# Decode with cached attention: nine VectorE instructions a head in place of fifteen

## The chip, the core and the metric

The kernel runs on one core of a Trainium2 chip. Its time is the device time of one execution, in microseconds (us). The runs of the kernel before took 715.30, 715.63 and 715.83 us: the median is 715.63 us. Lower is better.

In the text, PE is the matrix engine (TensorE), DVE is VectorE, ACT is ScalarE, POOL is GpSimd and SP is SyncE, which issues the loads here. A load is a DMA; 16 DMA engines carry it.

## The reference

One token for each of four sequences (B = 4) goes through two blocks, twice with the same weights: attention on a cache, then a dense MLP with ReLU. All is float32. Cut to what matters:

```python
def _A_ref(x, k_cache, v_cache, wq, wo):          # 32 heads of 128, window W = 1024
    q = (x @ wq).reshape(B, 1, 32, 128).transpose(0, 2, 1, 3)
    k = k_cache[:, :, Sk - W:, :]; v = v_cache[:, :, Sk - W:, :]
    p = softmax(einsum("bhqd,bhkd->bhqk", q, k) * 128 ** -0.5)
    o = einsum("bhqk,bhkd->bhqd", p, v)
    return o.transpose(0, 2, 1, 3).reshape(B, 1, 32 * 128) @ wo

def _B_ref(x, w1, w2):                            # 640 -> 1728 -> 640
    return einsum("bsf,fd->bsd", maximum(einsum("bsd,df->bsf", x, w1), 0), w2)

x = x + _A_ref(layernorm(x), ...);  x = x + _B_ref(layernorm(x), w1, w2)
x = x + _A_ref(layernorm(x), ...);  x = x + _B_ref(layernorm(x), w1, w2)
```

Each head of each pass needs its own part of `wq`, keys, values and its part of `wo`, 4.85 MB, and each is used for one token a sequence only. 302.7 MB are read from HBM in all.

## The kernel before, in words

**Records and slots.** The host packs what a head needs into one record of 9472 floats on each of 128 partitions: query weights (WQ, 640 columns), keys (K, 4096), values (V, 4096), output weights (WO, 640). On the chip five slots (`slot`) hold one record each; a buffer `ring` of 6912 columns holds MLP weights and some pieces of records between the two passes; `kept` holds a last part of one record. The small tiles (`qT`, `of_batch`, `of_block`, `pick`, `mrt`, `small`) are allocated ahead of the slots. Every tile starts at a multiple of 32 bytes in its partition; in the built program slot 0 starts at byte 3072, and the slots, the ring and `kept` at multiples of 256.

**Loads.** All weights are loaded by the SP queue, in one order that `items` holds, written out by hand (`piece`, `ending`, `IN_RING`, `places`). `pump` issues the next load as soon as the place that it overwrites has been marked as read by `done`; since the queue is in order, a load that must wait holds back those behind it. What frees a slot is the head's last use of it, `project`.

**The order of the work.** Every engine's instructions run in the order in which the code states them (`InOrder`). A pass `r` goes over 32 heads. `center` and `query` start it. Then, for each head `n`: `scores` of the next head (8 matrix products over 512 columns, on PE), its `softmax`, `values` of this head (8 products), `picks`, `query` of the head after next, `output_T`, `project` into the accumulator `acc`, and `weights` of the next head. The last heads of a pass stand outside the loop and work by halves. `busy` issues matrix products whose result is not used. Then `center` and `mlp`. In pass 0 the MLP's weights come through the ring: the fifth piece of `w1` overwrites the first, and the pieces of `w2` follow. In pass 1 they lie in two slots.

**VectorE's part of one head (15 instructions).** Four sequences stand on partitions 0, 32, 64 and 96. `softmax`: the row maximum over 1024 scores, its product with `rstd` (1/std of the layernorm); ScalarE then takes the exponential in place with `rstd` as scale, and the sum `tot`. `weights`: the sum is transposed, inverted and spread over the four columns of `mrt` (3 instructions); then, for each half of 512 columns, a transpose by blocks of 32 from `sc_ps` into `t_ps`, and a product that picks one column in each block, times `mrt`, into `wT` (4 instructions). `picks`: the values' product is a [128, 512] tile of which each row needs one of four blocks of 128; `of_block` holds a one in that block's column, and four instructions add the four blocks times their columns. Then the copies of the query (`qT`) and of the transposed output (`oTs`).

**1/std.** `deviation` sums the squares on PE, picks each row's value, sums and takes the root on ScalarE; in a pass it is issued behind the first half of the first head's scores, and in the MLP behind the first piece of `w1`.

In the profile every instruction but a few has line L89 (L86 for an engine's first): it is the line of the helper `InOrder` that calls the engine. So rows are told apart by their tiles.

Of the kernel before, what the change touches and what calls it, by code (L numbers as in the profile page):

```python
# [32 lines left out]
F32 = mybir.dt.float32  # L33
AF = mybir.ActivationFunctionType
OP = mybir.AluOpType
AX = mybir.AxisListType
PSUM = bass.MemoryType.PSUM

P = 128
B, D, H, DH, W, FF = 4, 640, 32, 128, 1024, 1728  # L40
# [56 lines left out]
def decode_kernel(ctx: ExitStack, tc: tile.TileContext, xf, rec, w1, w2, out):  # L97
    nc = tc.nc
    pe, dve, act, pool, sp = (InOrder(tc, e) for e in (nc.tensor, nc.vector, nc.scalar, nc.gpsimd, nc.sync))
    sb = ctx.enter_context(tc.tile_pool(name="sb", bufs=1))  # L100
# [4 lines left out]
    wT = scratch[:, :128].rearrange("p (i c j) -> p i c j", i=2, c=16)  # L105
    on = [scratch[:, 128:256], scratch[:, 288:416]]
# [5 lines left out]
    oTs = sb.tile([P, LATE, B], F32, name="oTs")  # L112
    qT = sb.tile([P, B], F32, name="qT")
    of_batch = sb.tile([P, B], F32, name="of_batch")
    of_block = sb.tile([P, 4], F32, name="of_block")
    pick = sb.tile([P, B], F32, name="pick")
    mrt = sb.tile([P, B], F32, name="mrt")
    small = sb.tile([P, 14], F32, name="small")
    nmax, rtot, rstd, eps, eps_dh, ones, unused, sums, tot0, tot1 = (small[:, i:i + 1] for i in range(10))
    squares = small[:, 10:]  # L120
    tot = [tot0, tot1]
# [4 lines left out]
    sc_ps = [ps.tile([P, W], F32, name=f"sc_ps{i}") for i in range(2)]  # L126
    t_ps = ps.tile([P, 512], F32, name="t_ps")
    o_ps = ps.tile([P, 512], F32, name="o_ps")
    acc = ps.tile([P, 512], F32, name="acc")
    misc = ps.tile([P, 512], F32, name="misc")  # L130
    outs = [o_ps, sc_ps[0][:, 512:]]
# [56 lines left out]
    hs = order[0]  # L188
# [13 lines left out]
    hs = order[1]  # L202
# [10 lines left out]
    for buf, lo, hi in places:  # L213
        while stream:
            h, c, end = stream[0]
# [11 lines left out]
    n = 0  # L227
# [18 lines left out]
    def cols(key, lo, n):  # L246

        for x, y, buf, col in pieces(key):
            if x <= lo and lo + n <= y:
                return buffers[buf][:, col + lo - x:col + lo - x + n]  # L250
        raise KeyError((key, lo, n))
# [39 lines left out]
        dve.tensor_tensor(spread[:, :KB * B].rearrange("p (k b) -> p k b", b=B), blocks, blocks, op=OP.mult)  # L291
        dve.tensor_reduce(squares, spread[:, :KB * B].rearrange("p (k b) -> p b k", b=B), op=OP.add, axis=AX.X)

    def deviation(rows, bias, scale):

        pe.matmul(o_ps[:, 8:8 + B], ones.to_broadcast([P, P]), squares, start=True, stop=True)
        dve.tensor_tensor(mrt, o_ps[:, 8:8 + B], rows, op=OP.mult)
        dve.tensor_reduce(sums, mrt, op=OP.add, axis=AX.X)
        act.activation(rstd, sums, AF.Sqrt, bias=bias, scale=scale / D)

    def xblock(k):
        return xT[:, 32 * k:32 * k + B]

    def query(r, h):
        key = ("rec", r, h)
        for k in range(KB):
            pe.matmul(misc[:, 8:8 + B], cols(key, WQ + k * DH, DH), xblock(k), start=(k == 0), stop=(k == KB - 1))
        done(key, WQ, K)
        dve.tensor_copy(qT, misc[:, 8:8 + B])

    def scores(r, h, s, first=False):
        key = ("rec", r, h)
        for i in range(2):
            for b in range(B):
                pe.matmul(sc_ps[s][32 * b:32 * b + 4, 512 * i:512 * i + 512], qT[:, b:b + 1].to_broadcast([P, 4]),
                          cols(key, K + 512 * (B * i + b), 512), start=True, stop=True)
            done(key, K + VH * i, K + VH * i + VH)
            if first and i == 0:
                deviation(of_batch, eps_dh, float(DH))
                act.activation(unused, eps, AF.Exp)  # L320

    def softmax(s, first=False):

        dve.tensor_reduce(nmax, sc_ps[s], op=OP.max, axis=AX.X, negate=True)
        if first:
            dve.reciprocal(rstd, rstd)
        dve.tensor_tensor(nmax, nmax, rstd, op=OP.mult)
        act.activation(sc_ps[s], sc_ps[s], AF.Exp, bias=nmax, scale=rstd, accum_out=tot[s])

    def weights(s, parts=(0, 1)):  # L330
        if 0 in parts:

            dve.transpose(spread, tot[s].to_broadcast([P, 32]))
            dve.reciprocal(rtot, spread[:, 0:1])
            dve.tensor_scalar(mrt, of_batch, rtot, None, op0=OP.mult)
        for i in parts:
            dve.transpose(t_ps, sc_ps[s][:, 512 * i:512 * i + 512])
            dve.tensor_tensor(wT[:, i], t_ps.rearrange("p (c j) -> p c j", j=32)[:, :, :B],
                              mrt.unsqueeze(1).to_broadcast([P, 16, B]), op=OP.mult)

    def values(r, h, last=False, fill=(0, 0)):
        key = ("rec", r, h)
# [6 lines left out]
                busy(512, misc)  # L349

    def picks(last):
        o, on_ = outs[last], on[last]
        dve.tensor_scalar(on_, o[:, :DH], of_block[:, 0:1], None, op0=OP.mult)
        for c in range(1, 4):
            dve.scalar_tensor_tensor(on_, o[:, DH * c:DH * c + DH], of_block[:, c:c + 1], on_, op0=OP.mult, op1=OP.add)

    def output_T(i, last=False, by_act=False):
        pe.matmul(outs[last][:, :B], on[last], pick, start=True, stop=True)
        if by_act:
            act.copy(oTs[:, i], outs[last][:, :B])  # L360
        else:
            dve.tensor_copy(oTs[:, i], outs[last][:, :B])

    def project(r, h, i, end):
        key = ("rec", r, h)
# [5 lines left out]
    def mlp(r):  # L371


        h_ps, front = sc_ps[0][:, :512], t_ps[:, :224]
        for k in range(KB):
            for j in range(NB):
                pe.matmul(h_ps[32 * j:32 * j + B, :FQ], xblock(k), cols(("w1", r), k * FF + FQ * j, FQ),
                          start=(k == 0), stop=(k == KB - 1))
            done(("w1", r), k * FF, k * FF + FF)
            if k == 0:  # L380
                deviation(pick, eps, 1.0)
                dve.reciprocal(rstd, rstd)
            elif k < KB - 1:
                busy(512)
        act.activation(front, h_ps[:, :224], AF.Relu, scale=rstd)
        act.activation(back[:, :208], h_ps[:, 224:FQ], AF.Relu, scale=rstd)
        act.activation(back[:, 240:], h_ps[:, 416:FQ], AF.Relu, scale=rstd)
        busy(512)
        busy(256)
        dve.transpose(scratch[:, :224], front)  # L390
        dve.transpose(scratch[:, 224:], back)
        key = ("w2", r)
        sizes = W2_SLOT if r else [size for name, size, _ in MLP_RING if name == "w2"]
        first = 0
        for i, size in enumerate(sizes):
            for s in range(first, first + size):
                m, n = TILES[s]
                w = cols(key, s * FD, FD)
                for part, q in ((m, n),) if m < 13 else ((13, n), (14, n + 2)):
                    pe.matmul(acc[32 * q:32 * q + B, :FD], hT[:, part, :B], w,  # L400
                              start=False, stop=(s >= len(TILES) - NB), skip_group_check=True)
            if r == 0 and i < len(sizes) - 2:
                busy(512)
            done(key, first * FD, (first + size) * FD)
            first += size
# [4 lines left out]
    for r in range(2):  # L410
        hs = order[r]
        late = LATE if r == 0 else 2
        center(2 * r)
        query(r, hs[0])
        if r:
            busy(256, groups=2)
        scores(r, hs[0], 0, True)
        softmax(0, True)
        query(r, hs[1])
        weights(0)  # L420
        for n, h in enumerate(hs[:-2]):
            i = n - (H - late)
            s = (n + 1) % 2
            scores(r, hs[n + 1], s)
            softmax(s)
            values(r, h)
            picks(0)
            query(r, hs[n + 2])
            if r and n < NS - 2:
                busy(256, sc_ps[n % 2], 2, H - 1)  # L430
            output_T(max(i, 0))
            if i < 0:
                project(r, h, 0, False)
            weights(s, (0, 1) if n < H - 3 else (0,))
        scores(r, hs[-1], 1)
        softmax(1)
        weights(0, (1,))
        values(r, hs[-2], 0, (0, 1))
        weights(1)
        picks(0)  # L440
        values(r, hs[-1], 1, (1, 0))
        output_T(late - 2, by_act=True)
        picks(1)
        for i in range(late - 3) if late > 2 else (0,):
            project(r, hs[H - late + i], i, False)
        if late == 2:
            busy(512, misc)
        output_T(late - 1, True)
        dve.memset(pad, 0.0)
        for i in (late - 3, late - 1, late - 2) if late > 2 else (1,):  # L450
            project(r, hs[H - late + i], i, i == late - 2 or late == 2)
        center(1)
        mlp(r)
# [40 lines left out]
```

## Time and profile before

| | before |
|---|---|
| runs, us | 715.30, 715.63, 715.83 |
| span of the profiled execution, us (its time around the span is not listed) | 713.9 |
| PE busy | 518.8 us (73%) |
| VectorE busy, instructions | 357.4 us (50%), 1007 |
| ScalarE busy, instructions | 93.3 us (13%), 147 |
| DMA | 303.38 MB, mean 425 GB/s over the span |
| mean granted clock of PE | 0.790 of full speed |

How to read it: the span runs from the first to the last instruction. A group's row has line, engine, operation, what it writes and reads, the shapes, and the count; then its busy time in us and the mean of one in ns; then the idle time of the engine just ahead of it and what ended that. A row of the timeline begins with its start and its length in us. A window's row has, for each engine, busy us and instructions, then PE's granted clock, the busy share of the 16 DMA engines, and GB/s. A row of waits has the total us, the number of waits and the longest. A row of the chain has a start, a length, and the work that the end of the program was waiting for at that time.

### The profile page before, as it was taken

The page shows a single profiled execution, that of the slowest core. Times are in us where ns is not written, and L with a number is a line of the kernel's source. Part 1 is how long each engine was busy: PE and PEld are TensorE (multiplying, and loading weights), DVE is VectorE, ACT ScalarE, POOL GpSimd, SP SyncE. Part 2 cuts the span into 40 slices and gives each one's busy share as a digit, 9 for nine tenths or more (in the row PEclk, how much of TensorE's full clock was granted, in tenths as well). Part 3 has the DMA queues.
Part 4 walks back from the last instruction along what each step waited for, and adds up shares of the span by engine and source line. Part 5 has one row for each costly group of instructions (what it writes and reads, how often), then busy time and mean ns, then how long its engine had stood idle before and what let it go on. Part 6 is the DMA issues. An engine that isn't in the chain of part 4 may idle for free.

```text
span 713.9 us, 8959 instructions
## 1 busy us (share of the span) xinstructions
PE 518.8 (73%) x3716; PEld 210.9 (30%) x3716; DVE 357.4 (50%) x1007; ACT 93.3 (13%) x147; POOL 1.1 (0%) x9
## 2 busy tenths in 40 slices
PE   4466858666785766868889998477767767686868
PEld 2131323223232231323224343132222313232323
DVE  3335445544454545446642887535444454445752
ACT  1201010110110101011111222101010110101111
POOL 0000000000000000000000000000000000000000
PEclk9768686877678677577899999857886687668989
DMA  9999999999999999999999999999999999999996
GB/s 374 442 437 430 425 436 440 429 419 442 438 432 423 434 438 437 417 442 422 424 406 408 428 429 429 442 438 423 430 439 436 427 430 434 437 430 423 429 424 274
DMA packets 16633, 303.38 MB, mean 425 GB/s; under 512 B 1856, under 2 KB 2384, under 8 KB 6736
## 3 DMA queue, kind: packets, MB, share of 16 engines
q1 hardware_dynamic: 16560, 302.80, 99.0%
q8 instruction: 29, 0.48, 0.2%
q14 instruction: 12, 0.10, 0.0%
q10 hardware_dynamic: 32, 0.01, 0.0%
HBM read 302.72 MB, written 0.08 MB: 424 GB/s over the span
## 4 chain that ended last, share of the span: by engine, by line
DMA 79%; PE 17%; DVE 2%; issue 1%; SPq 0%; ACT 0%
DMA slot<-rec 76%; PE sc_ps L89 6%; PE misc L89 5%; PE o_ps L89 4%; DMA ring<-w 3%; PE acc L89 3%; DVE scratch L89 1%; DVE oTs L89 1%; DVE small L89 0%; SPq L89 0%; DVE t_ps L89 0%; SPq L86 0%; DVE xT L89 0%; ACT oTs L89 0%; DVE qT L89 0%
## 5 line engine op out<-in xcount | busy, mean ns | idle before, releaser
L89 PE MATMUL misc<-xT,slot 128*128 128x4 f32 x630 | 103.2, 291 | 154.5 <-DMA slot<-rec 154.3
L89 PE MATMUL sc_ps<-slot,qT 128*4 128x512 f32 x1008 | 196.7, 920 | 1.0 <-DVE qT L89 1.0
L89 PEld LDWEIGHTS misc<-xT,slot 128*128 128x128 f32 x630 | 97.7, 240 | 210.8 <-DMA slot<-rec 199.1
L89 ACT ACTIVATE sc_ps<-sc_ps,small 128x1024 f32<-128x1024 f32 (+1 forms) x68 | 76.6, 1127 | 555.3 <-DVE small L89 554.8
L89 PE MATMUL o_ps<-slot,scratch 128*16 128x512 f32 x964 | 135.1, 672 | 3.0 <-DVE scratch L89 3.0
L89 DVE TENSOR_REDUCE small<-sc_ps 128x1 f32<-128x1024 f32 x64 | 78.3, 1223 | 73.9 <-PE sc_ps L89 73.9
L89 DVE STREAM_TRANSPOSE t_ps<-sc_ps 128x512 f32<-128x512 f32 x128 | 93.2, 728 | 2.1
L89 DVE COPY qT<-misc 128x4 f32<-128x4 f32 x64 | 10.2, 160 | 166.1 <-PE misc L89 166.1
L89 PEld LDWEIGHTS o_ps<-slot,scratch 128*16 128x16 f32 x964 | 32.7, 117 | 128.4 <-issue 79.0
L89 DVE SCALAR_TENSOR_TENSOR scratch<-o_ps,of_block,scratch 128x128 f32<-128x128 f32 x186 | 65.2, 351 | 6.6
L89 PEld LDWEIGHTS sc_ps<-slot,qT 128*4 128x4 f32 x1008 | 33.5, 115 | 84.1 <-issue 73.1
L89 PE MATMUL acc<-slot,oTs 128*4 128x160 f32 x488 | 36.5, 387 | 14.3 <-DVE oTs L89 14.0
L89 DVE TENSOR_SCALAR scratch<-o_ps,of_block 128x128 f32<-128x128 f32 x62 | 21.7, 351 | 34.1 <-PE o_ps L89 34.1
L89 PE MATMUL o_ps<-pick,scratch 128*128 128x4 f32 x124 | 29.1, 305 | 4.8 <-DVE scratch L89 4.8
L89 DVE TENSOR_TENSOR scratch<-t_ps,mrt 128x64 f32<-128x64 f32 x128 | 28.8, 225 | 4.7
L89 PEld LDWEIGHTS o_ps<-pick,scratch 128*128 128x128 f32 x124 | 26.1, 260 | 8.8 <-DVE scratch L89 7.5
L89 PE MATMUL sc_ps<-slot,small 128*1 128x256 f32 (+2 forms) x56 | 17.7, 462 | 0.0
L89 DVE COPY oTs<-o_ps 128x4 f32<-128x4 f32 x60 | 9.7, 162 | 14.8 <-PE o_ps L89 13.9
L89 DVE TENSOR_SCALAR mrt<-of_batch,small 128x4 f32<-128x4 f32 x64 | 14.7, 230 | 2.2
L89 DVE STREAM_TRANSPOSE scratch<-small 128x32 f32<-128x32 f32 x64 | 12.9, 201 | 2.4 <-ACT sc_ps L89 2.4
L89 PEld LDWEIGHTS acc<-slot,oTs 128*4 128x4 f32 x488 | 6.9, 84 | 19.5 <-DVE oTs L89 19.1
L89 ACT ACTIVATION_READ_ACCUMULATOR sc_ps<-sc_ps,small 128x1 f32 x64 | 12.2, 191 | 0.0
(71 smaller groups left out, 113.6 us busy)
## 6 DMA issues: line engine op xcount, KB each, us to landing
slot<-rec SPq DMA_DIRECT2D x43, 4736.0 KB, 30.7
slot<-rec SPq DMA_DIRECT2D x12, 2368.0 KB, 29.6
slot<-rec SPq DMA_DIRECT2D x2, 4416.0 KB
slot<-rec SPq DMA_DIRECT2D x2, 2304.0 KB, 18.4
ring<-w SPq DMA_DIRECT2D x5, 864.0 KB, 10.7
slot<-rec SPq DMA_DIRECT2D x2, 2112.0 KB, 19.0
slot<-rec SPq DMA_DIRECT2D x2, 2048.0 KB, 41.4
slot<-rec SPq DMA_DIRECT2D x4, 1024.0 KB, 20.3
```

The costliest lines, as they stand in the source:

```text
L89: r = build(*args, **kwargs)
```

## The change

Per head, VectorE gets 9 instructions where it had 15:

- `weights` transposes the whole row of 1024 in place in `sc_ps` and makes one product of all 32 blocks. The last two heads of a pass still go by halves, in place as well. `t_ps` is no longer used here.
- `picks` makes one product of the [128, 4, 128] view with `of_block`, in place in PSUM, and one sum over the four blocks.
- 1/std is multiplied into the query (`rrow`, one value a sequence, the same on all partitions) when it is copied to `qT`, for all heads of a pass but the first, whose query is copied ahead of the root. So the product on the row maximum falls away for them, and the exponential's scale is 1. `deviations` replaces `deviation` in attention: the root on four columns, its reciprocal, and the pick of each row's value for the first head.
- All copies to `oTs` are ScalarE's (before: two of them).

The new tile `rrow` has 16 bytes a partition and stands ahead of `small` and the slots. In the built program VectorE has 316 instructions fewer, its waits included, and ScalarE 60 more; PE's matrix products, their order, and the SP queue's loads are the same ones in the same order. The slots, the ring and `kept` start 32 bytes further.

```diff
+    rrow = sb.tile([P, B], F32, name="rrow")
     small = sb.tile([P, 14], F32, name="small")
...
+    def deviations():
+        pe.matmul(o_ps[:, 8:8 + B], ones.to_broadcast([P, P]), squares, start=True, stop=True)
+        act.activation(rrow, o_ps[:, 8:8 + B], AF.Sqrt, bias=eps_dh, scale=float(DH) / D)
+        dve.reciprocal(rrow, rrow)
+        dve.tensor_tensor(mrt, rrow, of_batch, op=OP.mult)
+        dve.tensor_reduce(rstd, mrt, op=OP.add, axis=AX.X)
...
-    def query(r, h):
+    def query(r, h, first=False):
...
-        dve.tensor_copy(qT, misc[:, 8:8 + B])
+        if first:
+            dve.tensor_copy(qT, misc[:, 8:8 + B])
+        else:
+            dve.tensor_tensor(qT, misc[:, 8:8 + B], rrow, op=OP.mult)
...
         dve.tensor_reduce(nmax, sc_ps[s], op=OP.max, axis=AX.X, negate=True)
         if first:
-            dve.reciprocal(rstd, rstd)
-        dve.tensor_tensor(nmax, nmax, rstd, op=OP.mult)
-        act.activation(sc_ps[s], sc_ps[s], AF.Exp, bias=nmax, scale=rstd, accum_out=tot[s])
+            dve.tensor_tensor(nmax, nmax, rstd, op=OP.mult)
+        act.activation(sc_ps[s], sc_ps[s], AF.Exp, bias=nmax, scale=rstd if first else 1.0, accum_out=tot[s])
...
-        for i in parts:
-            dve.transpose(t_ps, sc_ps[s][:, 512 * i:512 * i + 512])
-            dve.tensor_tensor(wT[:, i], t_ps.rearrange("p (c j) -> p c j", j=32)[:, :, :B],
-                              mrt.unsqueeze(1).to_broadcast([P, 16, B]), op=OP.mult)
+        for i, j in parts:
+            half = sc_ps[s][:, 512 * i:512 * j]
+            dve.transpose(half, half)
+            dve.tensor_tensor(wT[:, i:j].rearrange("p i c j -> p (i c) j"),
+                              half.rearrange("p (c j) -> p c j", j=32)[:, :, :B],
+                              mrt.unsqueeze(1).to_broadcast([P, 16 * (j - i), B]), op=OP.mult)
...
     def picks(last):
-        o, on_ = outs[last], on[last]
-        dve.tensor_scalar(on_, o[:, :DH], of_block[:, 0:1], None, op0=OP.mult)
-        for c in range(1, 4):
-            dve.scalar_tensor_tensor(on_, o[:, DH * c:DH * c + DH], of_block[:, c:c + 1], on_, op0=OP.mult, op1=OP.add)
+        o = outs[last].rearrange("p (c d) -> p c d", c=4)
+        dve.tensor_tensor(o, o, of_block.unsqueeze(2).to_broadcast([P, 4, DH]), op=OP.mult)
+        dve.tensor_reduce(on[last], o.rearrange("p c d -> p d c"), op=OP.add, axis=AX.X)
...
-        if by_act:
-            act.copy(oTs[:, i], outs[last][:, :B])
-        else:
-            dve.tensor_copy(oTs[:, i], outs[last][:, :B])
+        act.copy(oTs[:, i], outs[last][:, :B])
...
-            weights(s, (0, 1) if n < H - 3 else (0,))
+            weights(s, ((0, 2),) if n < H - 3 else ((0, 1),))
```

More of the change, by code (lines that the diff above doesn't have):

```diff
@@ L292, in center, with deviation @@
         dve.tensor_reduce(squares, spread[:, :KB * B].rearrange("p (k b) -> p b k", b=B), op=OP.add, axis=AX.X)
-    def deviation(rows, bias, scale):
+    def deviation():
         pe.matmul(o_ps[:, 8:8 + B], ones.to_broadcast([P, P]), squares, start=True, stop=True)
-        dve.tensor_tensor(mrt, o_ps[:, 8:8 + B], rows, op=OP.mult)
+        dve.tensor_tensor(mrt, o_ps[:, 8:8 + B], pick, op=OP.mult)
         dve.tensor_reduce(sums, mrt, op=OP.add, axis=AX.X)
-        act.activation(rstd, sums, AF.Sqrt, bias=bias, scale=scale / D)
+        act.activation(rstd, sums, AF.Sqrt, bias=eps, scale=1.0 / D)
+        dve.reciprocal(rstd, rstd)
+    def deviations():
[4 more added lines that the diff above has]
+        dve.tensor_reduce(rstd, mrt, op=OP.add, axis=AX.X)
     def xblock(k):
         return xT[:, 32 * k:32 * k + B]
-    def query(r, h):
+    def query(r, h, first=False):
         key = ("rec", r, h)
@@ L318, in scores @@
             if first and i == 0:
-                deviation(of_batch, eps_dh, float(DH))
+                deviations()
                 act.activation(unused, eps, AF.Exp)
@@ L325, in softmax, with weights @@
         if first:
-            dve.reciprocal(rstd, rstd)
-        dve.tensor_tensor(nmax, nmax, rstd, op=OP.mult)
-        act.activation(sc_ps[s], sc_ps[s], AF.Exp, bias=nmax, scale=rstd, accum_out=tot[s])
-    def weights(s, parts=(0, 1)):
-        if 0 in parts:
+            dve.tensor_tensor(nmax, nmax, rstd, op=OP.mult)
+        act.activation(sc_ps[s], sc_ps[s], AF.Exp, bias=nmax, scale=rstd if first else 1.0, accum_out=tot[s])
+    def weights(s, parts=((0, 2),)):
+        if parts[0][0] == 0:
             dve.transpose(spread, tot[s].to_broadcast([P, 32]))
@@ L351, in picks, with output_T @@
     def picks(last):
-        o, on_ = outs[last], on[last]
-        dve.tensor_scalar(on_, o[:, :DH], of_block[:, 0:1], None, op0=OP.mult)
-        for c in range(1, 4):
-            dve.scalar_tensor_tensor(on_, o[:, DH * c:DH * c + DH], of_block[:, c:c + 1], on_, op0=OP.mult, op1=OP.add)
-    def output_T(i, last=False, by_act=False):
+        o = outs[last].rearrange("p (c d) -> p c d", c=4)
+        dve.tensor_tensor(o, o, of_block.unsqueeze(2).to_broadcast([P, 4, DH]), op=OP.mult)
+        dve.tensor_reduce(on[last], o.rearrange("p c d -> p d c"), op=OP.add, axis=AX.X)
+    def output_T(i, last=False):
         pe.matmul(outs[last][:, :B], on[last], pick, start=True, stop=True)
-        if by_act:
-            act.copy(oTs[:, i], outs[last][:, :B])
-        else:
-            dve.tensor_copy(oTs[:, i], outs[last][:, :B])
+        act.copy(oTs[:, i], outs[last][:, :B])
     def project(r, h, i, end):
@@ L380, in mlp @@
             if k == 0:
-                deviation(pick, eps, 1.0)
-                dve.reciprocal(rstd, rstd)
+                deviation()
             elif k < KB - 1:
@@ L413, in decode_kernel @@
         center(2 * r)
-        query(r, hs[0])
+        query(r, hs[0], True)
         if r:
@@ L433, in decode_kernel @@
                 project(r, h, 0, False)
-            weights(s, (0, 1) if n < H - 3 else (0,))
+            weights(s, ((0, 2),) if n < H - 3 else ((0, 1),))
         scores(r, hs[-1], 1)
         softmax(1)
-        weights(0, (1,))
+        weights(0, ((1, 2),))
         values(r, hs[-2], 0, (0, 1))
-        weights(1)
+        weights(1, ((0, 1), (1, 2)))
         picks(0)
         values(r, hs[-1], 1, (1, 0))
-        output_T(late - 2, by_act=True)
+        output_T(late - 2)
         picks(1)
```

## The prediction

> **What bounds the kernel now.** I read the page first (the slices, the DMA queues), then the SP queue's waits and the chain that ended last, then windows and the timeline of the two places where that chain leaves the DMA.
>
> ```profile
> span 713.9 us, 8959 instructions
> DMA  9999999999999999999999999999999999999996
> DMA packets 16633, 303.38 MB, mean 425 GB/s; under 512 B 1856, under 2 KB 2384, under 8 KB 6736
> q1 hardware_dynamic: 16560, 302.80, 99.0%
> q8 instruction: 29, 0.48, 0.2%
> q14 instruction: 12, 0.10, 0.0%
> ...
> slot<-rec SPq DMA_DIRECT2D x43, 4736.0 KB, 30.7
> ```
>
> The 16 DMA engines are busy in every slice but the last, and the loads of q1 take 99.0% of their time. A whole record (4736 KB, 4.85 MB) needs 11.4 us at 425 GB/s but lands 30.7 us after its issue: some 19 us of other loads stand in front of it. So the order to load may come many microseconds later or earlier in the body without the DMA engines noticing.
>
> ```profile
> SPq L89 <- PE acc L89: 465.9, 51, 25.2
> ...
> 74.71 31.02 DMA slot<-rec
> ...
> 371.33 0.95 PE sc_ps L89 x8
> 372.30 7.20 DMA ring<-w
> ...
> 707.14 3.87 PE acc L89 x112
> 711.04 0.33 DVE scratch L89
> ```
>
> The first row (the SP queue's waits) says what issues loads: SP waits 465.9 us for a head's last projection, which frees its slot. The others are the chain: 31 us pieces of DMA through both passes of attention, a stretch between the two passes where the ring is fed by loads that land after only 7 us, and from 707 us on PE, DVE, the end. These two stretches are the places where VectorE could matter:
>
> ```profile
> core 0: us, PE busy (x) PEld busy (x) DVE busy (x) ACT busy (x) POOL busy (x), PEclk, DMA share, GB/s
> 369.00:372.00 3.00, 2.54 (x20) 0.51 (x20) 0.48 (x3) 1.58 (x2) 0.00 (x0) 1.00 0.93 364
> 372.00:375.00 3.00, 2.69 (x16) 0.36 (x11) 0.00 (x0) 0.00 (x0) 0.00 (x0) 1.00 0.99 402
> ...
> 706.00:708.00 2.00, 2.00 (x39) 1.24 (x41) 0.87 (x2) 1.02 (x3) 0.00 (x0) 1.00 0.53 220
> 708.00:710.00 2.00, 2.00 (x67) 1.90 (x61) 0.00 (x0) 0.00 (x0) 0.00 (x0) 1.00 0.28 108
> ```
>
> ```profile
> 667.83 1.90 PE L89 MATMUL sc_ps<-slot,qT 128*4 128x512 f32 x16
> ...
> 681.16 9.03 SPq L89 DMA_DIRECT2D slot<-w  x4
> ...
> 710.51 0.11 PEld L89 LDWEIGHTS acc<-slot,scratch 128*4 128x4 f32 x8 [0.18 <-DMA slot<-w]
> ```
>
> In 369 to 372 the DMA share falls to 0.93: the first MLP's fifth piece of w1 overwrites the first, so its load waits until PE has used that, and the queue runs nearly dry. At 7% of 3 us plus 1% of the next 3 this costs 0.24 us. At the end (the second and third row of the timeline) the last four loads are issued by 690.2, long before they are moved; their last piece reaches PE at 710.5, and PE has waited 0.18 us for it. DMA and PE end together there: the engines run out unevenly (shares 0.53 and 0.28). So an earlier PE gains next to nothing at the end, a PE later by x costs x minus 0.18.
>
> **The change, part by part.** Durations of the kinds it touches:
>
> ```profile
> L89 DVE STREAM_TRANSPOSE t_ps<-sc_ps 128x512 f32<-128x512 f32 x128 | 93.2, 728 | 2.1
> L89 DVE SCALAR_TENSOR_TENSOR scratch<-o_ps,of_block,scratch 128x128 f32<-128x128 f32 x186 | 65.2, 351 | 6.6
> L89 DVE TENSOR_TENSOR scratch<-t_ps,mrt 128x64 f32<-128x64 f32 x128 | 28.8, 225 | 4.7
> L89 DVE TENSOR_SCALAR scratch<-o_ps,of_block 128x128 f32<-128x128 f32 x62 | 21.7, 351 | 34.1 <-PE o_ps L89 34.1
> L89 DVE TENSOR_TENSOR small<-small 128x1 f32<-128x1 f32 x64 | 10.2, 159 | 2.2
> L89 DVE COPY oTs<-o_ps 128x4 f32<-128x4 f32 x60 | 9.7, 162 | 14.8 <-PE o_ps L89 13.9
> L89 ACT COPY oTs<-o_ps 128x4 f32<-128x4 f32 x2 | 0.3, 162 | 9.7 <-PE o_ps L89 9.7
> L89 DVE TENSOR_REDUCE scratch<-ring 128x128 f32<-128x512 f32 x1 | 1.0, 1023 | 0.3 <-POOL of_batch L89 0.3
> L89 DVE TENSOR_REDUCE small<-acc 128x1 f32<-128x160 f32 x4 | 1.3, 325 | 14.4 <-PE acc L89 9.5 <-PE acc L86 4.9
> ```
>
> 1. *Transposes and weights* (60 of 64 heads): two transposes and two products, 2 x 728 + 2 x 225 = 1.91 us, become one each. Products grow by 66 ns for 63 elements (159 to 225), so 128 elements take 0.29 us; a transpose of 1024 takes some 0.728 + 512 x 1.04 ns = 1.26 us (1.04 ns an element, from 325 ns for 160 and 159 for one). Together 1.55, 0.36 less. But PE's first four value products now wait for the whole row, 1.55 us rather than 0.95; the scores issued ahead of them cover that (1.90 us at full clock, the row at 667.83). Without this cover it would cost 0.6 us a head. The last two heads keep halves.
> 2. *Picks*: four instructions of 351 ns (1.40, with gaps 1.50 on the timeline) become a product over 512, 0.159 + 511 x 1.04 = 0.69 us, and a sum of 4 at a stride of 128. The sum's bounds: 0.325 + 352 x 1.04 = 0.69 us by the contiguous reductions, 1.23 us if a strided read costs two steps an element. I take 1.02, from the one reduction of the same size that reads with a stride. With a gap of 0.04 the pair is then 1.75: 0.25 *more* than now (bounds -0.08 and +0.46). Fewer instructions are not less work here.
> 3. *1/std in the query's copy*: the copy (160 ns) becomes a product of the same size (162); the product on the row maxima (159 ns, 62 heads) goes, and with its waits about 0.20 us from maximum to exponential. The root, its reciprocal and the pick happen once a pass, behind scores that PE is still computing: nothing.
> 4. *Copies by ScalarE*: 60 + 2 copies, 162 ns on either engine. The exponential ahead in ScalarE's queue is done by then; behind the copy waits only the next head's exponential. Nothing, in either direction, on PE's path; VectorE begins the next transpose some 0.2 us earlier.
>
> VectorE's sum: 60 x 0.36 + 62 x 0.16 + 62 x 0.16 - 64 x 0.25 = 25 us less busy. In the body all of it lies beside DMA. The cover there is the 19 us of queued loads.
>
> On the path at the end of pass 0:
>
> ```profile
> 356.44 1.23 DVE L89 TENSOR_REDUCE small<-sc_ps 128x1 f32<-128x1024 f32 x1 [1.50 <-PE sc_ps L89]
> 357.70 0.16 DVE L89 TENSOR_TENSOR small<-small 128x1 f32<-128x1 f32 x1
> ...
> 358.82 1.05 PE L89 MATMUL o_ps<-slot,scratch 128*16 128x512 f32 x8 [1.41 <-DVE scratch L89]
> ...
> 363.87 0.35 DVE L89 TENSOR_SCALAR scratch<-sc_ps,of_block 128x128 f32<-128x128 f32 x1 [0.41 <-PE sc_ps L89]
> 364.25 1.12 DVE L89 SCALAR_TENSOR_TENSOR scratch<-sc_ps,of_block,scratch 128x128 f32<-128x128 f32 x3
> 365.43 0.30 PEld L89 LDWEIGHTS sc_ps<-pick,scratch 128*128 128x128 f32 x2 [1.03 <-DVE scratch L89]
> ```
>
> The product at 357.70 goes: PE's values and all behind them come 0.20 us earlier (late next is the transpose behind it, as before). The last head's picks (363.87 to 365.37) cost 0.25 more. Sum +0.05 us (bounds -0.28 and +0.26) at the first MLP's start, which moves the dry spell at 369 by as much: 0.05. The end of pass 1 has the same two terms, +0.05, less PE's 0.18 of slack: 0 (bounds 0 and +0.08). Instructions fall by about 256 of 8959; of the 0.58 MB fetched on q8 and q14 that is 17 KB, two packets of q14: below 0.1 us on one DMA engine, taken as nothing.
>
> Two new things no row of before shows. The fetch order among DMA engines, and so which runs out last, may shift: up to 0.5 us either way, a quarter of the uneven finish (the 0.81 x 2 us of work left in 706 to 710 is spread over 4 us: over 2 us). And the new tile `rrow` stands ahead of the slots; tiles start at multiples of 32 bytes in the built program, so every slot, the ring and `kept` move from a multiple of 256 bytes (slot 0: 3072) to 32 past one (3104). Lower bound 0; the nearest rows are the two pieces of the ring that differ in this, before 377.7 us at a multiple of 256, after it 128 past one:
>
> ```profile
> 374.70:377.70 3.00, 2.66 (x22) 0.64 (x24) 0.49 (x2) 1.08 (x3) 0.00 (x0) 1.00 1.02 418
> 377.70:381.00 3.30, 3.10 (x46) 1.22 (x38) 0.37 (x1) 0.00 (x0) 0.00 (x0) 1.00 1.01 415
> ```
>
> 418 against 415 GB/s: at most 0.7% if the whole difference were the start, 5 us over the body; but their DMA shares differ by 1% too, so the likelier value is 0, which I take. The Trainium skill ("DMA: Bandwidth & Descriptors", How a descriptor splits into AXI transactions) says that a descriptor that starts off a 256-byte boundary begins its first transfer at the boundary below and pays for the unused bytes. By that rule, 32 bytes for each of some 920 data packets an engine would be an estimated 1.1 us and the sum 716.8; the same rule would ask 128 bytes in 7040 (11 tiles of 640), 1.8%, of the piece after 377.7, and the windows show less than half of that.
>
> Sum: 713.9 + 0.05 + 0 = 713.95 us of span, against 713.9. The runs' median is 715.63, so 1.7 us lie around the span, unchanged: **715.7 us**. No change that counts: 0.2%, 1.4 us, is about what a measurement of this kernel can tell from none.
>
> **Rivals.**
> *A, shifted slots slow the DMA.* For it: the DMA bounds everything and its every destination moves. Against: 418 beside 415. At 32 bytes a packet: 302.80 MB in 16560 - 1856 = 14704 packets, 919 an engine, each 32 bytes at 26.6 GB/s an engine = 1.2 ns: 1.1 us, 716.8. At the bound of 0.7%, 720.7. Slower by over 0.2% from 1.6 ns a packet on.
>
> *B, PE reaches the first MLP late, by its clock.*
>
> ```profile
> 393.00:396.00 3.00, 2.85 (x16) 0.46 (x16) 1.55 (x7) 1.29 (x2) 0.00 (x0) 0.56 1.01 410
> ...
> 393.15 3.46 PE L89 MATMUL sc_ps<-slot,qT 128*4 128x512 f32 x16 [0.50 <-DVE qT L89]
> ```
>
> Where the granted clock is 0.56, the 16 score instructions take 3.46 us, not 1.90: 1.56 more. If PE's new pattern of waits lost the clock once between 356 and 367 us, the first MLP would start 1.56 late, the dry spell would last as much longer, and the time would be 717.2: slower. It decides from 1.4 us of delay on. For it: here a wait of half a microsecond stands beside such a drop, and picks that are 0.25 longer make PE wait longer in the heads before. Against: PE's longest wait at this place (1.41 us) gets shorter by 0.20.
>
> *C, fewer instructions, not less work.* If product and sum both cost two steps an element (same bank read and written, strided read), the pair takes 1.23 + 1.23 + 0.04 = 2.5 us, 1.0 more than now; less the 0.20, that is 0.8 at the first MLP and 0.62 beyond the slack at the end: 717.1. For it: the strided reduction of 1023 ns. Against: the transpose reads and writes PSUM at one step an element.
>
> *D, faster.* Picks at their lower bound, -0.28, end the dry spell (0.24), and the DMA engines run out evenly by luck (2 us): 713.5. Each half alone stays within 0.2%.
>
> **How the numbers follow.** The forecast, 715.7, its own range 715.0 to 716.3: 0.62. A 0.12, half of it within 0.2%; B 0.12, of which 0.09 slower; C 0.08, of which 0.03 slower; D 0.06, of which 0.05 faster. That gives faster 0.05, same 0.77, slower 0.18. The range for 8 in 10 takes in A by one step a packet, B and C, and D's halves: 714.7 to 717.3.
>
> **What would show it.** Right: DMA share 1.0 throughout and 425 GB/s; VectorE some 25 us less busy; transposes of 1024 near 1.26 us; pair of picks between 1.4 and 2.0 us; SP's last loads issued some microsecond earlier or later with the same landing. Wrong: a mean rate under 423 GB/s (A); a share under 0.9 in the 3 us after the first MLP starts, with the clock under 1.0 before it (B) or a pair over 2.2 us (C); in the final MLP no wait of PE for the last piece, that is, PE ending alone. What would overturn the whole argument is a body in which DMA is not busy: a wait in PE's or ScalarE's queue that delays slots by more than 19 us.

## The result, and the profile after

The changed kernel takes 719.64 us (median of four runs, 719.40 to 719.89), the kernel before 715.61 beside it. The ratio is 1.0057, with a 95% interval of 1.0043 to 1.0071: 4.0 us slower. The prediction was 715.7, in a range to 717.3.

The page of the changed kernel:

```profile
span 717.8 us, 8700 instructions
PE 517.4 (72%) x3716; PEld 209.8 (29%) x3716; DVE 316.6 (44%) x635; ACT 97.8 (14%) x209; POOL 1.1 (0%) x9
DMA  9999999999999999999999999999999999999996
DMA packets 16631, 303.37 MB, mean 423 GB/s; under 512 B 1856, under 2 KB 2384, under 8 KB 6736
q1 hardware_dynamic: 16560, 302.80, 99.1%
q8 instruction: 29, 0.48, 0.3%
q14 instruction: 10, 0.08, 0.0%
```

The DMA engines are as busy as before (99.1%, before 99.0%) with the same 16560 packets and the same 302.80 MB, but the span is 3.9 us longer and the mean rate is 423 GB/s, not 425. VectorE is 40.8 us less busy. So the time did not go into idle DMA engines: the loads themselves take longer. The same is seen in the body alone; the windows of the kernel before, then of the changed one:

```profile
50.00:350.00 300.00, 217.16 (x1438) 87.50 (x1438) 150.40 (x416) 36.00 (x55) 0.00 (x0) 0.75 1.00 432
```

```profile
50.00:350.00 300.00, 213.64 (x1439) 87.21 (x1439) 131.48 (x251) 37.97 (x83) 0.00 (x0) 0.76 1.00 430
```

The DMA share is 1.00 in both and the rate 432 against 430 GB/s, with VectorE 19 us less busy. The groups that the change touches, of the changed kernel:

```profile
L89 DVE TENSOR_REDUCE small<-sc_ps 128x1 f32<-128x1024 f32 x64 | 78.4, 1225 | 124.6 <-PE sc_ps L89 124.6
L89 DVE STREAM_TRANSPOSE sc_ps<-sc_ps 128x1024 f32<-128x1024 f32 x60 | 75.5, 1258 | 0.0
L89 DVE TENSOR_TENSOR o_ps<-o_ps,of_block 128x512 f32<-128x512 f32 x62 | 43.4, 699 | 48.7 <-PE o_ps L89 42.2 <-ACT sc_ps L89 6.5
L89 DVE TENSOR_REDUCE scratch<-o_ps 128x128 f32<-128x512 f32 x62 | 42.9, 692 | 2.1
L89 DVE TENSOR_TENSOR scratch<-sc_ps,mrt 128x128 f32<-128x128 f32 x60 | 17.5, 292 | 2.1
L89 DVE TENSOR_REDUCE scratch<-ring 128x128 f32<-128x512 f32 x1 | 1.0, 1019 | 0.3 <-POOL of_batch L89 0.3
```

The transpose (1258 ns) and the product of 128 (292) came as worked out. The pair of picks takes 0.70 + 0.69 = 1.39 us, as long as the four instructions before. The end of the changed kernel, in its timeline and its windows:

```profile
712.00 2.00 PEld L89 LDWEIGHTS acc<-slot,scratch 128*4 128x4 f32 x60 [2.30 <-DMA slot<-w]
714.39 0.11 PEld L89 LDWEIGHTS acc<-slot,scratch 128*4 128x4 f32 x8 [0.39 <-DMA slot<-w]
```

```profile
706.00:708.00 2.00, 1.80 (x6) 0.32 (x4) 0.64 (x2) 1.08 (x3) 0.00 (x0) 1.00 0.97 406
708.00:710.00 2.00, 1.75 (x44) 1.23 (x44) 0.23 (x1) 0.00 (x0) 0.00 (x0) 1.00 0.85 348
710.00:712.00 2.00, 0.05 (x2) 0.00 (x0) 0.00 (x0) 0.00 (x0) 0.00 (x0) 1.00 0.55 227
```

PE waits 2.30 us and then 0.39 us for the last pieces of `w2`; the last piece reaches it at 714.39, 3.88 us later than before (710.51). The DMA share, 0.53 at 706 to 708 before, is 0.97 there now and falls to 0.55 at 710 to 712. The loads end 3.8 us later, and all behind them.

The trace's DMA records give the length of each packet. The packets of 37888 bytes (5504 of them, a whole record's row) took 1401 ns in 99% of cases before. After the change 4% do, 63% take 1404 to 1406 and 27% 1407 to 1413. That is what rival A asks for, destinations off their multiples of 256 bytes; the experiments test it.

### The profile page after: what moved, and what is told of

Read it like the earlier page. It is cut to its first block, busy times and chain, and to the rows that moved or that the text cites. A ratio compares the mean times of both kernels' runs of the same rounds, so it can differ in the third digit from the quotient of the medians.

```text
span 717.8 us, 8700 instructions
## 1 busy us (share of the span) xinstructions
PE 517.4 (72%) x3716; PEld 209.8 (29%) x3716; DVE 316.6 (44%) x635; ACT 97.8 (14%) x209; POOL 1.1 (0%) x9
## 3 DMA queue, kind: packets, MB, share of 16 engines
q1 hardware_dynamic: 16560, 302.80, 99.1%
## 4 chain that ended last, share of the span: by engine, by line
DMA 82%; PE 14%; DVE 1%; ACT 1%; issue 1%; SPq 0%; ACTq 0%; DVEq 0%
DMA slot<-rec 76%; PE misc L89 5%; PE sc_ps L89 4%; PE o_ps L89 4%; DMA ring<-w 3%; DMA slot<-w 3%; PE acc L89 2%; ACT oTs L89 1%; DVE scratch L89 1%; DVE o_ps L89 0%; DVE small L89 0%; ACT sc_ps L89 0%; DVE sc_ps L89 0%; SPq L89 0%; SPq L86 0%
## 5 line engine op out<-in xcount | busy, mean ns | idle before, releaser
L89 PE MATMUL o_ps<-slot,scratch 128*16 128x512 f32 x964 | 132.3, 662 | 4.1 <-DVE scratch L89 2.3
L89 ACT ACTIVATE sc_ps<-sc_ps,small 128x1024 f32<-128x1024 f32 (+1 forms) x68 | 71.1, 1046 | 311.6 <-DVE small L89 310.7
L89 DVE TENSOR_TENSOR qT<-misc,rrow 128x4 f32<-128x4 f32 x62 | 9.9, 160 | 163.6 <-PE misc L89 163.6
L89 DVE STREAM_TRANSPOSE sc_ps<-sc_ps 128x1024 f32<-128x1024 f32 (+1 forms) x68 | 81.3, 1195 | 0.1
L89 DVE TENSOR_TENSOR o_ps<-o_ps,of_block 128x512 f32<-128x512 f32 x62 | 43.4, 699 | 48.7 <-PE o_ps L89 42.2
L89 ACT COPY oTs<-o_ps 128x4 f32<-128x4 f32 x62 | 10.1, 162 | 250.5 <-PE o_ps L89 250.5
L89 DVE TENSOR_REDUCE scratch<-o_ps 128x128 f32<-128x512 f32 x62 | 42.9, 692 | 2.1
L89 DVE TENSOR_TENSOR scratch<-sc_ps,mrt 128x128 f32<-128x128 f32 (+1 forms) x68 | 19.3, 284 | 2.6
```

Source lines behind the costliest of these rows:

```text
L89: r = build(*args, **kwargs)
```

## The experiments

Unless said otherwise a kernel's time is its median, beside 715.57 to 715.62 us for the kernel before on the same chip.

**The change without the shift, and the shift without the change.** The first kernel allocates `rrow` behind `kept`. The second is the kernel before with an unused tile ahead of `small`.

```diff
-    rrow = sb.tile([P, B], F32, name="rrow")
     small = sb.tile([P, 14], F32, name="small")
...
     kept = sb.tile([P, REC - KEPT], F32, name="kept")
+    rrow = sb.tile([P, B], F32, name="rrow")
```

```diff
+    gap = sb.tile([P, 4], F32, name="gap")
     small = sb.tile([P, 14], F32, name="small")
```

> The changed kernel with `rrow` allocated behind `kept`: slots, ring and `kept` start again at multiples of 256 bytes (slot 0 at 3072), all instructions are those of the changed kernel. Theory S (the 4.0 us are the shift of every destination by 32 bytes): the packets of 37888 bytes take 1401 ns again, and the time is that of the kernel before, 715.4 to 715.9 us. Rival I (the 4.0 us come from the new instructions, such as longer waits of PE at the first MLP): 719.4 to 719.9, as the changed kernel. A time in between would split the 4.0 us between the two.

> The kernel before with an unused tile of 16 bytes where the change puts `rrow`: no instruction differs, only the addresses, which move 32 bytes. Theory S: 4 ns more for each of some 919 data packets an engine, 719.2 to 720.0 us. Rival I: 715.4 to 715.9.

Measured: 714.63 us (ratio 0.9984, 0.9975 to 0.9993) without the shift, 720.86 (1.0071, 1.0058 to 1.0083) with nothing but the shift. The shift costs 5.2 us in the kernel before (720.86 lies above the 719.2 to 720.0 that theory S gave) and 719.64 - 714.63 = 5.0 in the changed one. Theory S holds and rival I falls: the shift is more than the whole loss. The new instructions cost nothing; the change without the shift is 1.0 us *faster* than the kernel before, which no theory had expected. The page of the kernel with `rrow` behind `kept`:

```profile
span 712.8 us, 8700 instructions
DMA packets 16631, 303.37 MB, mean 426 GB/s; under 512 B 1856, under 2 KB 2384, under 8 KB 6736
q1 hardware_dynamic: 16560, 302.80, 99.2%
q14 instruction: 10, 0.08, 0.0%
```

and of the kernel before with the gap of 16 bytes:

```profile
span 719.1 us, 8959 instructions
DMA packets 16633, 303.38 MB, mean 422 GB/s; under 512 B 1856, under 2 KB 2384, under 8 KB 6736
q1 hardware_dynamic: 16560, 302.80, 98.9%
q14 instruction: 12, 0.10, 0.0%
```

The rate goes with the addresses: 426 and 425 GB/s at multiples of 256 bytes, 422 and 423 with the shift, with either set of instructions.

**How far off matters little.** The gap was made 128, 224 and 64 bytes (32, 56 and 16 columns).

> The kernel before with all destinations moved 128 bytes. If a packet off a multiple of 256 pays once, for one more stretch of 256 bytes that it touches (149, not 148, in 37888 bytes), the price is the same 4 ns as for 32 bytes and the time is 719 to 720.5 us. If it pays 4 ns for each 32 bytes that it is off, it takes 16 ns a packet and 730 us. If the position in 256 bytes plays no part but only that in 64 or 128 bytes, 715.6. In a sentence by itself: the Trainium skill (DMA: Bandwidth & Descriptors, How a descriptor splits into AXI transactions) has a descriptor pay for the bytes between the boundary below and its start, which at 1.2 ns for 32 bytes is an estimated 4.7 ns a packet here and 719.9 us.

> The kernel before with all destinations moved 224 bytes. One price for each packet that touches one more stretch of 256 bytes: 719 to 720.5 us again, the same as for 32 and for 128. A price that grows with the distance, 4 ns for each 32 bytes: 28 ns a packet, 741 us. In a sentence by itself: by the rule of the Trainium skill named at the kernel moved 128 bytes, 7 times 1.2 ns a packet, an estimated 8.2 ns and 723.2 us, against an estimated 716.7 for 32 bytes.

> The kernel before with all destinations moved 64 bytes. 32 and 224 bytes cost 5.2 and 5.4 us, 128 bytes 4.1. If all odd starts pay the same two parts (3 to 4 ns for one more stretch of 256 bytes, and 7 ns more in a fifth of the packets), 720.9; if the second part goes with starts that are not multiples of 64, or of 128, bytes, 719.7 or 720.9.

Measured, with the lengths of packets from the trace's DMA records (the kernel before and its gaps; the columns are the bytes that destinations stand past their old places, the median and mean length of packets of 37888 bytes and the part of them at 1401 ns or less, the median length of the 128 packets of 8064 bytes, and the time):

```
past   37888 B: median  mean  <=1401   8064 B: median   time, us
  0             1401   1403.4   99%             305      715.6
 32             1405   1408.6    4%             305      720.86
 64             1404   1407.6   12%             305      720.16
128             1405   1407.1   27%             305      719.69
224             1405   1408.7    4%             312      721.05
```

The price does not grow with the distance: 224 bytes cost what 32 cost, not seven times as much. Two times lie outside what was expected: 721.05 us, a little above 720.5, and 720.16 us for 64 bytes, between the values named. For a packet the price is nearly the same at several sizes (medians at 0 and at 32 bytes past: 18944 bytes 705 and 708 ns, 8192 bytes 309 and 313, 4096 bytes 159 and 162); at 2048 bytes the median does not move (84 and 84).

Whether it is the price of one more stretch of 256 bytes that a packet touches is not shown. The packets of 8064 bytes are 31.5 stretches: they touch 32 when they start 0, 32, 64 or 128 bytes past a multiple and 33 at 224, and there alone their median is longer. But at 32 past, too, only 57% of them still take 305 ns, where it was 98%. And in the kernel before one piece, of 6656 bytes (26 stretches), starts 128 bytes past a multiple and so touches 27: 125 of its 128 packets take 253 ns, as do 112 of them where the gap of 128 bytes puts it on a multiple. An off piece among aligned ones pays nothing there.

The Trainium skill (DMA: Bandwidth & Descriptors, How a descriptor splits into AXI transactions) names the boundary of 256 bytes, and the runs agree that it matters. A price by the bytes ahead of the start, which the page says are fetched unused, does not fit these runs: by it 32 bytes would be an estimated 1.2 ns a packet and 224 an estimated 8.2, and both measured 5.2 to 5.3 ns in the mean. The page does not say whether it holds for the writing side, and it is the destinations that moved here. Open is why 64 and 128 bytes cost 0.7 and 1.2 us less than 32: more of their packets keep 1401 ns, and no run told which ones.

**Which multiple, and whose price.** In the kernel before, slots 0 and 1 were moved 256 bytes and all behind them 288.

```diff
+    gap = sb.tile([P, 64], F32, name="gap")
     small = sb.tile([P, 14], F32, name="small")
...
-    slot = [sb.tile([P, REC], F32, name=f"slot{i}") for i in range(NS)]
+    slot = [sb.tile([P, REC], F32, name=f"slot{i}") for i in range(2)]
+    gap2 = sb.tile([P, 8], F32, name="gap2")
+    slot += [sb.tile([P, REC], F32, name=f"slot{i}") for i in range(2, NS)]
```

> The kernel before with unused tiles, so that slots 0 and 1 start 256 bytes further (at 3328, an odd multiple of 256) and slots 2 to 4, the ring and `kept` 288 bytes further. If what counts is only whether a destination starts at a multiple of 256 bytes and each packet pays by its own destination, the packets of 37888 bytes split: about two in five take 1401 ns as before, the others 1404 to 1412, and the time is 715.6 + 0.6 x 5.2 (the price of the 32 bytes alone, 720.86 less 715.62) = 718.7 us. If a multiple of 512 is needed, none take 1401 ns and it is 720.9. If the price is one of the program as a whole (some table or queue), all packets are alike: 715.6 or 720.9.

Measured: 718.70 us (718.66 to 718.73), where 718.7 was expected of a price by destination. But the packets did not split as expected: 62% of those of 37888 bytes take 1401 ns or less, not two in five, 24% take 1404 to 1406 and 10% 1407 to 1413. The DMA records, put in order of their starts and counted off 128 to a record, say which slots they go to:

```
slot  past a multiple of 256   <=1401 ns
 0             0                  83%
 1             0                 100%
 2            32                  97%
 3            32                  28%
 4            32                   9%
```

The slots are filled in this order, over and over. So a start at an odd multiple of 256 is free (slot 1, and slot 0 but for its first packets), and the price is not one of the program as a whole. But a packet does not simply pay for its own destination: slot 2 is off and keeps 1401 ns behind two slots that are not, and the first packets into slot 0 still pay behind slots 3 and 4. The same is seen in the kernel with the gap of 16 bytes: of the 128 packets of each of its first four whole records, all of them 32 bytes past, 117, 96, 17 and 0 keep 1401 ns. The price shows about one record behind its cause. Why is open, and as the packets of whole records carry 38% of the price (2.0 of 5.2 ns) and not 60%, the match of the time is in part luck.

**The 1.0 us that the change gains.** Without the shift the changed kernel fetches 10 packets of instructions on q14 in the span, the kernel before 12. Useless stores were added to it until VectorE's instructions were as many as before; twice as many; or as much time in few instructions.

```diff
             weights(s, ((0, 2),) if n < H - 3 else ((0, 1),))
+            if n < H - 3:
+                for _ in range(5 + n % 2):
+                    dve.memset(spare, 0.0)
```

The second has `range(2 * (5 + n % 2))`, the third one `dve.memset(t_ps[:, :256], 0.0)` in place of the loop. Two more kernels make one part of the change alone in the kernel before: the functions `picks` and `weights` of the diff.

> The changed kernel with `rrow` behind `kept` (714.63 us, 1.0 less than before) and 319 instructions of VectorE added that do nothing of use (a store of one column, behind the weights of 58 heads), so that the number of instructions that VectorE fetches is that of the kernel before. Theory F (the 1.0 us is instruction fetch: two packets fewer on the fetch queue, 10 in place of 12 in the span, and the last DMA engine then ends 1.7 us behind the mean of the 16 in place of 2.6): 12 packets again and 715.3 to 715.9 us. Rival P (the 1.0 us is a path, PE's earlier work at the end of a pass or at the first MLP): 714.4 to 714.9.

> The changed kernel with `rrow` behind `kept` and 638 useless instructions of VectorE, twice as many as before (715.62 us with 319, 714.63 with none). Theory F (each packet of 8 KB on the fetch queue, 128 instructions, costs about 0.5 us at the end): 14 or 15 packets, 2 to 3 more than with 319, and 716.3 to 717.2 us. Rival P2 (319 brought back 715.6 only because the time of the kernel before is a level of its own, or because of the DMA engine that the packets happen to fall on): 715.3 to 715.9, or any other value without a step of 0.5 us a packet.

> The changed kernel with `rrow` behind `kept`, and in place of the 319 short stores one store of 256 columns in PSUM behind the weights of 58 heads: VectorE is busy for about as long as with the 319 (58 x 0.25 us = 14.5 us, beside 318 x 59 ns = 18.8 us) with a fifth of the instructions. Theory F: 10 or 11 packets of fetch, 714.5 to 715.1 us. Rival T (the 1.0 us is VectorE's time, not its instructions): 715.4 to 715.8.

> The kernel before with the new picks alone (one product, one strided sum); all destinations at multiples of 256 bytes. 124 instructions fewer than before. The pair should take 0.70 + 0.69 us, as in the changed kernel, in place of 1.40: nothing on the path. Theory F: one packet of fetch fewer or none, 715.0 to 715.7. Rival P: 0.05 us at each end of a pass, 715.5 to 715.6.

> The kernel before with the whole-row transposes in place alone; all destinations at multiples of 256 bytes. 120 instructions fewer. PE's first four value products of a head wait for the whole row (1.55 us, not 0.95); that lies under the scores issued ahead of them, so nothing on the path. Theory F: one packet of fetch fewer or none, 715.0 to 715.7. Rival P: 715.6; if the longer wait shows, each pass's end would be later by up to 0.6 us, 716.2.

Measured (all with destinations at multiples of 256 bytes; the packets are q14's in the span; the last columns, from the DMA records, say when the 16 engines end their loads in the mean, and when the last one does):

```
kernel                           q14   time, us   ends: mean    last
change, rrow behind kept          10    714.63       707.41   709.12
  as long, in few instructions    10    714.75       707.27   709.31
before, weights alone             11    715.01       707.69   709.72
before, picks alone               11    714.94       707.56   709.43
before                            12    715.6        707.55   710.14
change + 319 instructions         12    715.62       707.78   709.99
change + 638 instructions         15    718.42       708.46   712.56
```

The groups of the added stores, first with 319, then in few instructions:

```profile
L89 DVE MEMSET spare<- 128x1 f32 x318 | 18.8, 59 | 18.1
```

```profile
L89 DVE MEMSET t_ps<- 128x256 f32 x58 | 15.8, 272 | 3.0
```

With 319 instructions added the gain is gone (ratio 1.0002, 0.9993 to 1.0011). With nearly as much of VectorE's time in 58 instructions it stays (0.9984, 0.9975 to 0.9993). So rival T falls, and rival P, as long as it counts VectorE's work: what counts is the number of instructions fetched, theory F. Each part alone sheds one packet and lies between, picks alone a little below the 715.0 named (both ratios 0.9994, 0.9985 to 1.0003, by themselves not to be told from 1). What is gained is at the end: from 12 packets to 10 the mean end moves by 0.14 us, the last one by 1.02. The windows of the kernel with `rrow` behind `kept` show it beside the rows of before in the prediction (0.53, 0.28):

```profile
706.00:708.00 2.00, 0.83 (x27) 0.65 (x31) 0.00 (x0) 0.00 (x0) 0.00 (x0) 1.00 0.52 216
708.00:710.00 2.00, 1.92 (x52) 1.06 (x40) 0.01 (x1) 0.00 (x0) 0.00 (x0) 1.00 0.19 71
```

The doubled stores cost more than expected, 718.42 us: 0.5 us a packet from 10 to 12, 0.9 from 12 to 15, where a packet of q14 itself takes 0.31 us in the records. The records show what comes on top. They don't name the engine of a packet, but packets follow each other at a fixed step (one starts 3 or 4 ns ahead of the end of another), and such packets are taken here as those of one engine. In the kernel before, seven q14 packets have a packet of 37888 bytes right behind them: five of these take 1932 to 1987 ns and two 1647 and 1651 ns, not 1401. A fetch thus holds its engine for 0.6 to 0.9 us, mostly 0.84. And followed back by this step from the end of the last load (within 9 ns, at one place 18), every chain that fits goes through q14 packets, at 664.5, 569.9 and 474.0 us in the kernel before, at 568.4, 479.4 and 415.2 us with 319 stores, and at 710.4 and 503.5 us with 638: there the last engine is one that carries such fetches. Three more at 0.84 us, if all are on it, are 2.5 us; the last end moved by 2.57.

Two things stay open. From 10 to 12 packets the last end moves by 1.02 us only, not 1.7, and in the kernels with 10 or 11 the last engine was not traced in this way. With 638 there is a second effect: the engines' mean end is 0.9 us later than before's, so part of the loss is in the loads ahead of the end.

The fastest kernel of all is the change with `rrow` behind `kept`: 714.63 us against 715.62 (ratio 0.9984).

## Why the prediction was wrong

The step that failed is the tile `rrow`: "so the likelier value is 0, which I take". It measured +5.0 us, the upper bound of that step (5 us) and not its lower. The mechanism stood there as rival A with 0.12. That the bound came out as large as the price is luck, for the rows under it do not show the price. The row beside it, 415 against 418 GB/s, compares a piece that starts 128 bytes past a multiple with one on a multiple, but the packets of both (7040 bytes) take 267 ns in the kernel before: a single off piece among aligned ones does not pay, as with the piece of 6656 bytes above. And a rate over 3 us, rounded to 1 GB/s, is no measure of 4 ns in 1401. The lengths of the packets are the finer measure, in the kernel before one length to the nanosecond in 99% of those of 37888 bytes; but no whole record starts off a multiple there, so no row of before could give the price, and none spoke for 0. Rival A's own price, one step of 32 bytes or 1.2 ns a packet (716.8 us), was too small by a factor of four.

The rest, point by point:

- *DMA sets the time, the body does not feel VectorE.* Right. VectorE became 40.8 us less busy, and the kernel with the change but not the shift is 1.0 us faster, for which fetch accounts. Between the passes, where PE runs without waiting for loads, a head takes as long with the change as without, in the one pair compared. PE's timeline, first of the kernel before, then of the change with `rrow` behind `kept`, one head after the other:

```profile
413.43 1.90 PE L89 MATMUL sc_ps<-slot,qT 128*4 128x512 f32 x16
419.59 1.90 PE L89 MATMUL sc_ps<-ring,qT 128*4 128x512 f32 x16
```

```profile
413.70 1.90 PE L89 MATMUL sc_ps<-slot,qT 128*4 128x512 f32 x16
419.90 1.90 PE L89 MATMUL sc_ps<-ring,qT 128*4 128x512 f32 x16
```

  6.16 and 6.20 us, so VectorE was not the bound there either.

- *Transposes and weights*, 1.26 and 0.29 us: 1258 and 292 ns. Right.
- *Picks*, 1.75 us with bounds of 1.42 and 1.96: it took the lower bound, as the timeline of the changed kernel has it (1.41 us from the product's start to the sum's end):

```profile
363.60 0.69 DVE L89 TENSOR_TENSOR o_ps<-o_ps,of_block 128x512 f32<-128x512 f32 x1
364.32 0.69 DVE L89 TENSOR_REDUCE scratch<-o_ps 128x128 f32<-128x512 f32 x1
```

  The row from which I took 1.02 for the sum is still there with 1019 ns; it reads SBUF, through a pattern of more dimensions, so its time was not the price of a stride alone. VectorE therefore saves 40.8 us, not 25. It moved nothing in the time. Rival C falls.
- *1/std and copies by ScalarE*: nothing on the path. Right; copies take 162 ns on ScalarE too.
- *The path at the first MLP*, +0.05, and the end, 0: nothing that counts. Without the shift the DMA share there is nearly as before, in the windows of the change with `rrow` behind `kept`:

```profile
369.00:372.00 3.00, 3.00 (x25) 0.94 (x22) 0.48 (x3) 0.29 (x1) 0.00 (x0) 1.00 0.89 330
372.00:375.00 3.00, 2.52 (x16) 0.32 (x18) 0.00 (x0) 0.00 (x0) 0.00 (x0) 1.00 0.99 404
```

  0.89 and 0.99, before 0.93 and 0.99: 4% of 3 us, 0.1 us more. A share under 0.9 was named as a sign of B or C, but B needs a clock under 1.00, which it is not here, and C a pair over 2.2 us. Rival B falls.
- *Instruction fetch*: "two packets of q14: below 0.1 us on one DMA engine, taken as nothing". The count was right (12 to 10), the price wrong: 1.0 us. I spread the packets' bytes over all the DMA, but a packet takes 0.31 us on its one engine, the load behind it gets longer by 0.25 to 0.59 us in the kernel before, and the end is set by the last of 16 engines. The uneven end, which I gave "0.5 us either way" as a matter of luck, follows the fetches.

With both sizes put right the sum gives the result: 715.6 + 5.0 - 1.0 = 719.6, measured 719.64. As the 5.0 was taken from that same result, this checks nothing by itself; with the shift as measured in the kernel before, 5.2, the sum is 719.9, 0.2 off.

## What to carry to other kernels

In a kernel bound by DMA, look at where each loaded tile starts: a small tile allocated ahead of the large ones can move every destination off its multiple of 256 bytes, which here was 4 to 5 ns a packet and 0.7% of the time; put small tiles behind the loaded ones, or fill up to 256. Read a price of that size from the lengths of single packets, not from rates of windows, and ask of a comparison whether it holds the case that pays. Where the end is the last DMA engine's, count the packets of instructions too, and look at the load right behind each.

## What the runs showed of the hardware

With all destinations at multiples of 256 bytes, 99% of the packets of 37888 bytes take 1401 ns; with all of them 32 or 224 bytes past one, 4% do, and most take 1404 to 1413. The price shows late: behind two slots at (odd) multiples, 97% of the packets into a slot 32 bytes past one still took 1401 ns. Instructions that wait for nothing are not free beside loads that fill the DMA engines: each packet of 8 KB of them, some 128 of VectorE's (638 added, 5 packets more), cost 0.5 to 0.9 us here, for it takes 0.31 us and the load behind it on its engine mostly 0.53 us more, while 15.8 us of VectorE's time in 58 instructions cost 0.1, which is within the spread of the runs.
